# H3 convolution layer with a squared-ReLU MLP on one core: a normalisation moved one step, side jobs of the convolution placed anew, SyncE's transfers held back to three in flight

## The chip, the core and the metric

The kernel runs on one core of a Trainium2 chip. The core has TensorE (PE in the profile; PEld is its weight load), VectorE (DVE), ScalarE (ACT), GpSimd (POOL) and SyncE (SP, which here only issues transfers). The engines run side by side, each through its own list of instructions in order, and wait for each other by semaphores. The metric is the device time of one execution in microseconds, as the median of several runs.

## The reference, cut to what matters

S = 2048 positions, D = 640 channels, F = 1728 hidden units, float32.

```python
mod = (silu(c) @ w_mod)            # six rows of 640: sa, ca, ga, sb, cb, gb
h  = layernorm(x) * (1 + ca) + sa
k_shift = causal_conv(k, shift_k)  # 4 taps per channel
kv = k_shift * v
y  = irfft(rfft(kv, 4096) * rfft(ssm_k, 4096))[:2048] + kv * ssm_D
x  = x + ga * (h * y)              # the long convolution, gated with h
h  = layernorm(x) * (1 + cb) + sb
x  = x + gb * (relu(h @ w1 + b1) ** 2 @ w2 + b2)
```

## The kernel before, in words

**The convolution** takes the channels in five blocks of 128 (b = 0 to 4). The long convolution is a Fourier transform of 4096 points, done as matmuls with constant tables. For each block TensorE runs units of work:

- kv_k, kv_v (L232, L270): transposes of k and v to channels by time, in four pieces of 512. kv_s (L253) applies the taps on VectorE, kv_m (L281) multiplies by v and stores the piece to kv_d in DRAM.
- load_h, load_x (L205, L213): four transfers each bring kv (from kv_d) and ssm_k into the tile p, in another layout.
- unit_a (L374), eight for each block: the first stage of the transform, 64 small matmuls each, "pa" in the profile; four read the ssm_k part of p (i = 1), four the kv part (i = 0). ScalarE copies the result to the tile a.
- front (L421), eight steps j: the second stage for ssm_k (h) and kv (x), the product of the spectra on VectorE (tile wx), sums on GpSimd. back (L449), "qp", turns two steps back.
- unit_t and unit_y (L524, L534), eight each: transposes t and the last inverse stage y, into the tile up.

**Side jobs** are done for the blocks before and after, between these units: the modulation rows (part_load, part_scale, part_add, mod_row, mod_col: load a 128 by 640 piece of w_mod, scale it on ScalarE, add on GpSimd, sum with a matmul by ones), the statistics of the first normalisation (q_big loads q, stats1, stats1_end), the normalised and modulated input (load_xp, prep_a on ScalarE, prep_m on VectorE, prep_p on GpSimd), the gate, the residual (finish_near, finish_add, which stores to x1_d), and the first MLP weights (load_item, w_high on ScalarE, w_low: a weight is split into a high and a low part).

**The order is written out by hand.** A block has ten steps FS(b, 0) to FS(b, 9), with the fronts and backs, and 18 slots GS(b, 0) to GS(b, 17) (11 in the last block). The table filled by at (L890) says which side jobs are called in which step or slot. UNITS (L1069) gives for each block the slots of unit_a for the next block (one more stands in step 9), of unit_t and of unit_y. AFTER (L1067) lists the steps and slots in which the side jobs and the next unit_a change places: normally a slot calls its unit_a first and its side jobs then, in AFTER the other way round. keep_order (L118) ties each engine's instructions to the order in which the program made them.

**Transfers** nearly all go through sp_dma (L137): SyncE issues them in program order, and each waits until the one OUT = 4 places ahead has landed. The pieces of w_mod and the MLP weights share four buffers (tag STG).

**The MLP** goes through 8 chunks n of 256 positions and 14 steps f each (128 hidden units a step). A pass of the main loop at (n, f) calls, in this order: mlp_back of the step three passes ago (MLAG = 3; second matmul, "acc"), mlp_split of the last step (high part on ScalarE, L146, low part on VectorE, L157), mlp_front (first matmul, "h", L720), mlp_front_end (ReLU on ScalarE, L752, the square on GpSimd), and then the work for chunk n + 1: load_x1 at f = 3, stats2 at 5, stats2_root and stats2_end at 6, prep_hat (L670, its ScalarE instruction at L672) and, from f = 8 on, prep_xt, which transposes one block of channels a step (L685, two transposes, one for each half of the chunk, "xtp") and makes its high and low parts. prep_hat(n + 1, i) normalises half i of the next chunk into the tile xh[i] ("mtmp" in the profile); it is called for i = 0 at f = 7 and i = 1 at f = 8, for n = 0 at 5 and 6. xh is also the buffer in which mlp_end and mlp_out scale and add a chunk's result, at f = 2.

Of the kernel before, what the change touches and what calls it, by code (L numbers as in the profile page):

```python
# [28 lines left out]
OUT = 4  # L29
# [63 lines left out]
def ssm_mlp_kernel(  # L93
# [796 lines left out]
    def at(i, *calls):  # L890
        tab[i] += calls
# [45 lines left out]
    def b2_load():  # L937
# [3 lines left out]
    at(FS(0, 1), (kv_k, 1, 0, "T"), (kv_v, 1, 0), (p_tile, 2))  # L941
    at(FS(0, 2), (early_h, 0, 6))
    at(FS(0, 3), (kv_s, 1, 0))
    at(FS(0, 4), (early_h, 0, 7))
    at(FS(0, 5), (kv_m, 1, 0), (kv_k, 1, 1, "T"))
    at(FS(0, 6), (skip, 1))
    at(FS(0, 7), (kv_s, 1, 1))
# [3 lines left out]
    at(GS(0, 1), (kv_s, 1, 2))  # L951
    at(GS(0, 2), (stats1, 0))
    at(GS(0, 3), (kv_m, 1, 2), (kv_k, 1, 3, "X"), (kv_s, 1, 3))
    at(GS(0, 5), (kv_v, 1, 3), (kv_m, 1, 3), (kv_k, 2, 0, "X"), (stats1, 4))
    at(GS(0, 6), (stats1, 1), (mod_start,))
    at(GS(0, 7), (stats1, 2), (part_load, 2, 0), (part_load, 2, 1), (part_load, 2, 2))
    at(GS(0, 8), (load_x, 1), (kv_s, 2, 0), (q_big, "X1", 8))
    at(GS(0, 9), (kv_v, 2, 0), (kv_k, 2, 1, "Y"), (stats1, 3))
    at(GS(0, 11), (kv_m, 2, 0), (stats1, 5))
    at(GS(0, 12), (q_big, "X1", 10))  # L960
    at(GS(0, 13), (kv_s, 2, 1), (kv_v, 2, 1), (kv_m, 2, 1))
    at(GS(0, 14), (load_h, 2), (stats1, 6))
    at(GS(0, 15), (part_load, 2, 3))
    at(FS(1, 0), (part_scale, 2, 1))
    at(FS(1, 1), (kv_k, 2, 2, "T"), (q_big, "UP1", 12), (stats1, 7))
    at(FS(1, 2), (part_scale, 2, 0))
    at(FS(1, 3), (skip, 2), (kv_s, 2, 2), (kv_v, 2, 2), (kv_m, 2, 2), (kv_k, 2, 3, "T"), (part_add, 2, 1, pool))
    at(FS(1, 4), (kv_s, 2, 3), (kv_v, 2, 3), (part_scale, 2, 2), (part_load, 2, 4))
    at(FS(1, 5), (kv_m, 2, 3), (part_add, 2, 2, pool), (part_scale, 2, 3), (part_load, 1, 0))
    at(FS(1, 6), (q_ut,))  # L970
    at(FS(1, 7), (part_add, 2, 3, pool))
    at(FS(1, 8), (load_xp, 0))
    at(FS(1, 9), (load_x, 2), (stats1, 13), (part_scale, 2, 4))
    at(GS(1, 0), (p_tile, 3), (kv_k, 3, 0, "Y"))
    at(GS(1, 1), (kv_s, 3, 0), (part_load, 1, 1))
    at(GS(1, 2), (kv_v, 3, 0), (part_scale, 1, 0))
    at(GS(1, 3), (kv_m, 3, 0), (part_add, 2, 4, pool), (part_load, 1, 2))
    at(GS(1, 4), (kv_k, 3, 1, "Y"), (stats1, 12), (part_load, 1, 4))
    at(GS(1, 5), (kv_v, 3, 1), (stats1, 14), (mod_row, 2), (part_scale, 1, 1), (part_load, 1, 3))
    at(GS(1, 7), (kv_s, 3, 1), (stats1, 15), (part_add, 1, 1, pool))  # L980
    at(GS(1, 8), (kv_k, 3, 2, "Y"))
    at(GS(1, 9), (kv_m, 3, 1), (kv_s, 3, 2), (part_scale, 1, 2), (part_scale, 1, 4), (part_load, 0, 2))
    at(GS(1, 10), (kv_v, 3, 2))
    at(GS(1, 11), (kv_k, 3, 3, "Y"), (stats1, 9), (part_scale, 1, 3), (part_load, 0, 0))
    at(GS(1, 12), (stats1, 11), (part_add, 1, 4, pool), (part_load, 0, 1))
    at(GS(1, 13), (kv_m, 3, 2), (kv_s, 3, 3), (part_add, 1, 2, pool))
    at(GS(1, 14), (kv_v, 3, 3), (part_add, 1, 3, pool))
# [8 lines left out]
    at(FS(2, 4), (part_add, 0, 4, pool), (prep_a, 0, 0), (prep_a, 0, 3), (prep_m, 0, 1))  # L996
    at(FS(2, 5), (prep_m, 0, 0))
    at(FS(2, 6), (skip, 3), (part_load, 3, 0), (part_load, 3, 2), (prep_a, 0, 2), (prep_m, 0, 3))
    at(FS(2, 7), (mod_row, 0), (prep_p, 0, 0), (prep_p, 0, 1))
    at(FS(2, 8), (prep_m, 0, 2))  # L1000
    at(FS(2, 9), (part_load, 3, 1), (prep_p, 0, 2), (prep_p, 0, 3), (gate, 0, 0))
    at(GS(2, 0), (kv_k, 4, 0, "Y"), (part_scale, 3, 0))
    at(GS(2, 1), (kv_s, 4, 0), (part_scale, 3, 1), (gate, 0, 1))
    at(GS(2, 2), (p_tile, 4), (load_h, 4), (part_load, 3, 3), (gate, 0, 3), (finish_add, 0, 1))
    at(GS(2, 3), (kv_v, 4, 0), (kv_m, 4, 0), (kv_k, 4, 1, "Y"), (kv_v, 4, 1))
    at(GS(2, 4),
        (part_scale, 3, 2), (part_load, 3, 4), (gate, 0, 2), (finish_near, 0, 0), (finish_near, 0, 1),
        (finish_add, 0, 2), (finish_add, 0, 3), (prep_a, 1, 0),
    )
# [36 lines left out]
    at(GS(3, 13), (mod_col, 4, cbs[:, 1], 1.0), (prep_m, 3, 2), (prep_p, 3, 2))
    at(GS(3, 15), (prep_m, 3, 1), (prep_p, 3, 1), (w_tile, "S0", 3), (w_low, dve))
    at(GS(3, 16), (w_high,))
    at(GS(3, 17), (prep_a, 3, 3), (w_low, dve))
    at(FS(4, 0), (prep_m, 3, 3), (load_item,), (load_item,))  # L1050
    at(FS(4, 1), (prep_p, 3, 3), (gate, 3, 1), (gate, 3, 2))
    at(FS(4, 2), (gate, 3, 0), (u_tile, 4), (prep_a, 4, 0), (prep_m, 4, 0), (w_high,))
    at(FS(4, 3), (gate, 3, 3), (prep_a, 4, 1))
    at(FS(4, 4), (prep_m, 4, 1), (prep_p, 4, 0), (w_high,))
    at(FS(4, 5), (gate_load,), (load_item,))
    at(FS(4, 6), (prep_a, 4, 2), (w_low, dve))
    at(FS(4, 7), (prep_m, 4, 2), (prep_p, 4, 1))
    at(FS(4, 8), (w_tile, "S2", 3), (w_high,), (w_high,))
    at(FS(4, 9), (finish_add, 3, 1), (w_tile, "S3", 3), (load_item,), (load_item,), (w_low, dve))
    at(GS(4, 0), (prep_a, 4, 3), (prep_m, 4, 3), (prep_p, 4, 2), (prep_p, 4, 3))  # L1060
    at(GS(4, 2), (finish_near, 3, 0), (finish_near, 3, 1), (finish_add, 3, 2))
    at(GS(4, 3), (b2_load,), (w_low, pool), (w_low, pool))
    at(GS(4, 4), (load_item,))
# [203 lines left out]
```

## Time and profile before

| | us |
|---|---|
| median of 3 runs | 703.28 |
| lowest, highest | 702.06, 704.84 |
| profiled execution | 705.5 |
| its span, first to last instruction | 703.7 |

The profile describes one execution. The convolution takes some 285 us of the span and the MLP the rest. A row of the timeline gives start, duration, engine, source line, operation, tiles written and read, shapes, how many alike, and in brackets how long the engine stood idle before it and what ended that. A row of waits gives who waited for whom, the total, how often and the longest. "issue" names idle time that nothing in the profile ended. q1 is the queue of SyncE's transfers, q8 carries instructions (packets, MB, share of the DMA engines' time). Ends of matmuls are modelled, so idle times of TensorE are good to some tenths of a microsecond.

### The profile page before, as it was taken

What the parts mean: (1) busy time and instruction counts of PE and PEld (TensorE: products, weight loads), DVE (VectorE), ACT (ScalarE), POOL (GpSimd) and SP (SyncE); (2) the same over time, 40 slices, a digit from 0 to 9 for tenths busy, and PEclk for the clock granted to TensorE, in tenths of its full rate; (3) what the DMA queues carried; (4) which work ended last, traced back from release to release, by engine and by line L of the source; (5) the groups of instructions that cost most, each with busy time, mean ns of one, the idle gap of its engine ahead of it and who ended that gap; (6) DMA issues with size and microseconds to landing.
All of it is one profiled execution on the core that took longest, in us unless ns stands there. A gap on an engine that the chain in (4) does not pass through costs nothing.

```text
span 703.7 us, 21084 instructions
## 1 busy us (share of the span) xinstructions
PE 662.0 (94%) x9164; PEld 634.2 (90%) x9164; DVE 334.6 (48%) x601; ACT 329.6 (47%) x688; POOL 311.2 (44%) x390
## 2 busy tenths in 40 slices
PE   6699799999999989999999999999999999999997
PEld 5688788888898888899999999999999999999996
DVE  5257666657684886587522323323332322422313
ACT  4436556877967966566233333233233233233221
POOL 1053155459869859433514414315215215224213
PEclk9999999999999999999999999999999999999999
DMA  9887889798672645274010100200200200200001
GB/s 232 248 240 235 238 238 250 232 231 219 181 186 82 158 126 172 69 227 142 39 38 1 42 35 1 74 3 1 75 1 1 76 1 1 76 1 1 38 1 38
DMA packets 110960, 74.76 MB, mean 106 GB/s; under 512 B 48658, under 2 KB 96146, under 8 KB 110868
## 3 DMA queue, kind: packets, MB, share of 16 engines
q1 hardware_dynamic: 108912, 72.87, 36.5%
q8 instruction: 72, 1.18, 0.7%
q10 hardware_dynamic: 1892, 0.54, 0.3%
q14 instruction: 20, 0.16, 0.1%
q0 software_dynamic: 64, 0.01, 0.0%
HBM read 58.98 MB, written 14.42 MB: 104 GB/s over the span
## 4 chain that ended last, share of the span: by engine, by line
PE 83%; ACT 6%; DVE 5%; issue 3%; DMA 2%; POOL 1%; SPq 0%; DVEq 0%; ACTq 0%; POOLq 0%
PE acc L790 27%; PE h L720 25%; PE pa L383 5%; PE x L398 5%; PE qp L464 5%; PE y L541 5%; PE h L398 3%; PE t L530 2%; PE h L711 1%; PE xtp L685 1%; PE kt L239 1%; DVE wx L151 1%; ACT a L146 1%; PE vt L276 1%; PE gr L928 1%
## 5 line engine op out<-in xcount | busy, mean ns | idle before, releaser
L151 POOL TENSOR_TENSOR mtmp<-mtmp 128x256 f32<-128x256 f32 x112 | 71.4, 638 | 244.4 <-ACT mtmp L752 236.5
L720 PE MATMUL h<-xt,w_S 128*128 128x256 f32 x1290 | 167.5, 281 | 1.1 <-DVE w_S L157 1.1
L720 PEld LDWEIGHTS h<-xt,w_S 128*128 128x128 f32 x1290 | 161.7, 190 | 1.3 <-DVE w_S L157 1.3
L790 PE MATMUL acc<-w_S,hring 128*128 128x320 f32 x960 | 156.6, 311 | 0.2 <-DVE hring L157 0.2
L157 DVE TENSOR_TENSOR hring<-mtmp,hring 128x256 fp32r<-128x256 f32 x112 | 66.4, 593 | 162.6 <-ACT hring L146 162.6
L790 PEld LDWEIGHTS acc<-w_S,hring 128*128 128x128 f32 x960 | 142.0, 188 | 0.7 <-DVE hring L157 0.7
L752 ACT ACTIVATE mtmp<-h,b1t 128x256 f32<-128x256 f32 x104 | 49.4, 475 | 180.1 <-PE h L720 177.0
L146 ACT ACTIVATE hring<-mtmp 128x256 fp32r<-128x256 f32 x112 | 46.6, 416 | 48.5 <-POOL mtmp L151 47.5
L383 PE MATMUL pa<-wx,p 64*64 64x64 f32 x2560 | 49.7, 228 | 10.9 <-issue 5.3
L383 PEld LDWEIGHTS pa<-wx,p 64*64 64x64 f32 x2560 | 44.1, 141 | 17.2 <-issue 11.3
L146 ACT ACTIVATE a<-pa 128x512 f32<-128x512 f32 x80 | 43.6, 611 | 22.9 <-PE pa L383 22.8
L151 DVE TENSOR_TENSOR wx<-x,wx 128x512 f32<-128x512 f32 x64 | 41.0, 684 | 19.4 <-PE x L398 8.9
L541 PE MATMUL y<-wx,wx 128*64 128x64 f32 x1280 | 45.4, 226 | 4.5 <-ACT wx L146 2.7
L541 PEld LDWEIGHTS y<-wx,wx 128*64 128x64 f32 x1280 | 40.7, 139 | 9.5 <-issue 4.2
L687 DVE TENSOR_SCALAR we<-xtp,cbs 128x256 f32<-128x256 f32 x35 | 19.0, 544 | 61.1 <-PE xtp L685 61.1
L398 PE MATMUL x<-a,gb 128*64 128x128 f32 x640 | 43.8, 281 | 3.0 <-DVE wx L151 1.8
L398 PEld LDWEIGHTS x<-a,gb 128*64 128x64 f32 x640 | 37.7, 141 | 4.4 <-PE h L398 2.4
L261 DVE SCALAR_TENSOR_TENSOR KV<-kt,tap,KV 128x511 f32<-128x511 f32 (+2 forms) x48 | 35.9, 747 | 8.1 <-ACT ktail L146 6.3
L154 POOL TENSOR_TENSOR wm<-wm,wm 128x640 f32<-128x640 f32 x20 | 32.9, 1647 | 10.3 <-ACT wm L341 10.0
L146 ACT ACTIVATE q<-qp 128x512 f32<-128x512 f32 (+1 forms) x40 | 21.3, 585 | 33.1 <-PE qp L464 33.1
L157 POOL TENSOR_TENSOR we<-wx 128x256 f32<-128x256 f32 x20 | 15.8, 789 | 47.0 <-DVE wx L151 46.1
L398 PE MATMUL h<-a,gb 128*64 128x128 f32 x512 | 34.4, 275 | 0.6 <-ACT wx L146 0.6
(142 smaller groups left out, 1032.7 us busy)
## 6 DMA issues: line engine op xcount, KB each, us to landing
wm<-in_w_mod_dram SPq DMA_DIRECT2D x25, 320.0 KB, 4.2
KV<-in_A_k_dram SPq DMA_DIRECT2D x20, 256.0 KB, 4.6
KV<-in_A_v_dram SPq DMA_DIRECT2D x20, 256.0 KB, 4.5
p<-in_A_ssm_k_dram SPq DMA_DIRECT2D x20, 256.0 KB, 4.9
p<-kv_d SPq DMA_DIRECT2D x20, 256.0 KB, 4.8
xp<-in_A_q_dram SPq DMA_DIRECT2D x20, 256.0 KB, 4.5
q<-in_A_q_dram SPq DMA_DIRECT2D x15, 320.0 KB, 5.0
out_dram<-x SPq DMA_DIRECT2D x14, 320.0 KB, 2.2
```

What stands on the lines that cost most here:

```text
L146: act.activation(o, i, AF.Copy)
L151: eng.tensor_mul(o, a, b)
L154: eng.tensor_add(o, a, b)
L157: eng.tensor_sub(o, a, b)
L261: dve.scalar_tensor_tensor(o, tk[:, : 512 - t], tap[:, b, t : t + 1], o, op0=ALU.mult, op1=ALU.add)
L383: pe.matmul(t[e][64 * r : 64 * r + 64, g].rearrange("p m d -> p (m d)"), pt[b][l, i, 8 * q + g, :], cw[l, r], start=True, stop=True,)
L398: pe.matmul(t[64 * a : 64 * a + 64, s + r], gb[:, g, r, a], AX[b][i][:, 2 * g + a], start=True, stop=True,)
L464: pe.matmul(t[a][:, u], gi[l, 4 * j + u, r], w[r][l, u % 2], start=(r == 0), stop=(r == 1),)
L541: pe.matmul(y[64 * h : 64 * h + 64, 4 * (g % 2) + i].rearrange("p c l d -> p (c l d)"), tss[g][:, i, 64 * r : 64 * r + 64], ca[:, r, h], s ...
L720: pe.matmul(hps[n, f][:m], WI[1, f][:, a, b], XT[n][:, x, b], start=(b == 0 and i == 0), stop=(b == NB - 1 and i == 2),)
L752: act.activation(r[:m], h[:m], AF.Relu, bias=b1t[:m, f : f + 1])
L790: pe.matmul(acc[2 * s + i], h[:, a, s * P : (s + 1) * P], w[:, y, i * 320 : (i + 1) * 320], start=(f == 0 and ti == 0), stop=(f == NF - 1 ...
```

## The change

Three things. (1) OUT is 3: each of SyncE's transfers waits for the third one ahead. (2) In the MLP, for n of 1 and more, both calls of prep_hat stand at f = 7; for n = 0 they stay at 5 and 6. (3) The table of side jobs, UNITS and AFTER are new. All side jobs are still called once each; with them their transfers move in SyncE's order. The diff, cut to its core (of the table those lines that are spoken of below, lines with other jobs of the same step included):

```diff
-OUT = 4
+OUT = 3
...
-    at(FS(0, 8), (kv_v, 1, 1))
-    at(FS(0, 9), (q_big, "XP0", 0))
-    at(GS(0, 0), (kv_m, 1, 1), (kv_k, 1, 2, "Y"), (kv_v, 1, 2), (q_big, "XP1", 4))
+    at(FS(0, 5), (skip, 1), (kv_k, 1, 1, "T"), (q_big, "XP0", 0))
+    at(GS(0, 0), (kv_v, 1, 1), (kv_m, 1, 1), (kv_k, 1, 2, "Y"), (kv_v, 1, 2))
+    at(GS(0, 2), (q_big, "XP1", 4))
...
-    at(FS(1, 8), (load_xp, 0))
-    at(FS(1, 9), (load_x, 2), (stats1, 13), (part_scale, 2, 4))
+    at(GS(1, 1), (load_x, 2), (kv_s, 3, 0), (part_load, 1, 1))
...
-        (kv_m, 3, 3), (stats1, 8), (stats1, 10), (mod_row, 1), (part_scale, 0, 0), (part_scale, 0, 1),
-        (part_scale, 0, 2), (part_load, 0, 3), (part_load, 0, 4),
+        (kv_v, 3, 3), (kv_m, 3, 3), (mod_row, 1), (part_scale, 0, 0), (part_scale, 0, 1), (part_scale, 0, 2),
     )
-    at(GS(1, 16), (load_x, 3), (stats1_end,), (part_add, 0, 1, pool), (part_add, 0, 2, pool))
-    at(FS(2, 0), (load_h, 3), (load_xp, 1))
-    at(FS(2, 2), (part_scale, 0, 3), (prep_a, 0, 1))
-    at(FS(2, 3), (part_add, 0, 3, pool), (part_scale, 0, 4))
+    at(GS(1, 16), (stats1, 8), (part_add, 0, 2, pool), (part_load, 0, 4))
+    at(GS(1, 17), (load_h, 3), (stats1, 10), (load_xp, 1))
+    at(FS(2, 0), (load_x, 3), (part_scale, 0, 3))
+    at(FS(2, 1), (stats1_end,), (part_add, 0, 1, pool), (part_add, 0, 3, pool), (prep_a, 0, 1))
+    at(FS(2, 2), (part_scale, 0, 4))
...
-    at(FS(4, 0), (prep_m, 3, 3), (load_item,), (load_item,))
-    at(FS(4, 2), (gate, 3, 0), (u_tile, 4), (prep_a, 4, 0), (prep_m, 4, 0), (w_high,))
-    at(FS(4, 4), (prep_m, 4, 1), (prep_p, 4, 0), (w_high,))
+    at(GS(3, 17), (prep_p, 3, 1), (u_tile, 4), (w_low, dve), (load_item,))
+    at(FS(4, 2), (gate, 3, 0), (prep_a, 4, 1), (prep_m, 4, 0), (w_high,), (w_high,))
...
     UNITS = [
-        ([0, 2, 4, 11, 11, 16, 16], [1, 3, 3, 5, 5, 6, 7, 9], [3, 4, 4, 6, 6, 8, 9, 10]),
-        ([1, 1, 5, 7, 9, 10, 12], [1, 3, 4, 6, 8, 11, 14, 14], [4, 6, 7, 10, 13, 14, 16, 17]),
+        ([0, 1, 4, 11, 13, 16, 16], [1, 3, 3, 5, 5, 6, 7, 9], [3, 4, 4, 6, 7, 8, 8, 11]),
+        ([2, 2, 5, 5, 10, 10, 12], [1, 4, 4, 7, 8, 11, 13, 14], [4, 7, 7, 11, 13, 13, 16, 17]),
...
-                if f - (5 if n == 0 else 7) in (0, 1):
-                    prep_hat(n + 1, f - (5 if n == 0 else 7))
+                if n == 0 and f in (5, 6):
+                    prep_hat(1, f - 5)
+                if n and f == 7:
+                    prep_hat(n + 1, 0)
+                    prep_hat(n + 1, 1)
```

AFTER goes from 20 places to 27. In the built program the new order gives TensorE of block 1 three pairs of unit_a with nothing between them (slots 2, 5 and 10), where there was one (slot 1).

More of the change, by code (lines that the diff above doesn't have):

```diff
@@ new lines, in ssm_mlp_kernel @@
+    at(GS(0, 2), (q_big, "XP1", 4))
+    at(GS(0, 3), (kv_m, 1, 2), (kv_k, 1, 3, "X"), (kv_s, 1, 3), (stats1, 4))
+    at(GS(0, 5), (kv_v, 1, 3), (kv_m, 1, 3), (kv_k, 2, 0, "X"), (stats1, 1))
+    at(GS(0, 6), (stats1, 3), (mod_start,), (part_load, 2, 0))
+    at(GS(0, 7), (kv_s, 2, 0), (stats1, 2), (part_load, 2, 2))
+    at(GS(0, 8), (load_x, 1))
+    at(GS(0, 9), (kv_v, 2, 0), (stats1, 5), (part_load, 2, 1))
+    at(GS(0, 10), (kv_k, 2, 1, "Y"))
+    at(GS(0, 11), (kv_m, 2, 0), (kv_s, 2, 1), (q_big, "X1", 8))
@@ L1059, in ssm_mlp_kernel @@
[L1059 to L1063, printed above, removed]
-    at(GS(4, 5), (finish_add, 3, 3), (gate_vector,), (load_item,))
-    AFTER = {GS(0, 9), GS(0, 11), GS(0, 14), GS(1, 1), GS(1, 4), GS(1, 12), GS(1, 13), GS(1, 14), FS(2, 9), GS(2, 1), GS(2, 2), GS(2, 9), GS(2, 10), GS(2, 15), GS(2, 17), GS(3, 2), GS(3, 5), GS(3, 10), GS(3, 12), GS(3, 16)}
@@ L1069, in ssm_mlp_kernel @@
-    UNITS = [
[5 rows of a table removed]
+    at(GS(2, 9), (kv_s, 4, 2), (kv_v, 4, 2), (part_add, 3, 2, pool), (part_add, 3, 3, pool))
+    at(GS(2, 10), (load_xp, 2), (prep_m, 1, 1))
+    at(GS(2, 11), (kv_k, 4, 3, "Y"), (part_scale, 3, 4))
+    at(GS(2, 12), (part_add, 3, 4, pool), (prep_p, 1, 1), (prep_a, 1, 2))
+    at(GS(2, 13), (kv_m, 4, 2), (kv_s, 4, 3), (kv_v, 4, 3))
+    at(GS(2, 14), (kv_m, 4, 3))
+    at(GS(2, 15),
+        (mod_col, 3, cbs[:, 0], 0.0), (prep_m, 1, 2), (prep_a, 1, 3), (prep_m, 1, 3), (prep_p, 1, 3),
+        (gate, 1, 0),
+    )
@@ new lines, in ssm_mlp_kernel @@
+    at(GS(2, 16), (part_load, 4, 3), (prep_p, 1, 2), (gate, 1, 1))
+    at(GS(2, 17), (part_load, 4, 1))
+    at(FS(3, 0), (part_load, 4, 2), (finish_near, 1, 1), (prep_a, 2, 0))
+    at(FS(3, 1), (part_load, 4, 0), (gate, 1, 2), (finish_near, 1, 0))
+    at(FS(3, 2), (load_x, 4), (finish_add, 1, 2))
+    at(FS(3, 3), (skip, 4))
+    at(FS(3, 4), (part_scale, 4, 0), (gate, 1, 3), (prep_m, 2, 0), (prep_p, 2, 0))
+    at(FS(3, 5), (finish_add, 1, 1))
+    at(FS(3, 6), (part_scale, 4, 1), (part_scale, 4, 2))
@@ new lines, in ssm_mlp_kernel @@
+    at(FS(3, 7), (prep_a, 2, 1))
+    at(FS(3, 8), (part_add, 4, 2, pool), (gate, 2, 0))
+    at(FS(3, 9), (part_scale, 4, 3), (prep_m, 2, 1))
+    at(GS(3, 1), (part_add, 4, 1, pool), (finish_add, 1, 3), (prep_p, 2, 1))
+    at(GS(3, 2), (part_load, 4, 4), (prep_a, 2, 2))
+    at(GS(3, 3), (prep_m, 2, 2), (prep_a, 2, 3), (finish_near, 2, 0), (w_tile, "S1", 3))
+    at(GS(3, 4), (part_add, 4, 3, pool), (load_xp, 3), (prep_p, 2, 2))
+    at(GS(3, 5), (prep_m, 2, 3), (prep_p, 2, 3), (gate, 2, 1), (finish_near, 2, 1))
@@ new lines, in ssm_mlp_kernel @@
+    at(GS(3, 6), (load_item,))
+    at(GS(3, 7), (load_item,))
+    at(GS(3, 8), (part_scale, 4, 4))
+    at(GS(3, 9), (part_add, 4, 4, pool), (gate, 2, 2), (finish_add, 2, 2), (prep_a, 3, 0), (b1_load,))
+    at(GS(3, 10), (finish_add, 2, 1), (prep_a, 3, 2), (load_item,))
+    at(GS(3, 11), (prep_m, 3, 0), (w_high,))
+    at(GS(3, 12),
+        (mod_col, 4, cbs[:, 1], 1.0), (gate, 2, 3), (finish_add, 2, 3), (load_xp, 4), (prep_p, 3, 0),
+        (prep_a, 3, 1),
+    )
+    at(GS(3, 13), (prep_m, 3, 2))
@@ new lines, in ssm_mlp_kernel @@
+    at(FS(4, 5), (prep_m, 4, 1))
+    at(FS(4, 6), (prep_a, 4, 2), (gate_load,))
+    at(FS(4, 7), (prep_m, 4, 2), (prep_p, 4, 1))
+    at(FS(4, 8), (finish_add, 3, 1), (w_tile, "S3", 3), (w_high,))
+    at(FS(4, 9), (prep_a, 4, 3), (prep_p, 4, 2), (w_tile, "S2", 3), (w_low, dve))
+    at(GS(4, 0), (prep_m, 4, 3), (prep_p, 4, 3))
+    at(GS(4, 1), (finish_add, 3, 2), (load_item,), (load_item,), (w_high,))
+    at(GS(4, 2), (finish_near, 3, 0), (finish_near, 3, 1))
+    at(GS(4, 3), (b2_load,))
```

156 lines of the change are left out of this document (61 added, 95 removed), and 6 rows, old and new, of the table UNITS.

## The prediction, as put on record before the run

> **What bounds the kernel now.** I read the page first: its busy shares, the slices, the chain that ended last.
>
> ```profile
> span 703.7 us, 21084 instructions
> PE 662.0 (94%) x9164; PEld 634.2 (90%) x9164; DVE 334.6 (48%) x601; ACT 329.6 (47%) x688; POOL 311.2 (44%) x390
> ...
> DMA  9887889798672645274010100200200200200001
> ...
> q8 instruction: 72, 1.18, 0.7%
> ...
> PE 83%; ACT 6%; DVE 5%; issue 3%; DMA 2%; POOL 1%; SPq 0%; DVEq 0%; ACTq 0%; POOLq 0%
> ```
>
> TensorE carries the chain almost alone, so a change is worth what it does to TensorE's waits. Transfers fill the first third of the span and nearly vanish later. The profiled execution took 705.5 us, 1.8 more than its span; the median of the runs shown is 703.28 (702.06 to 704.84). I make the sum on the 705.5 and subtract it from the median as well.
>
> Second view: who waited for whom on TensorE, in two stretches. First 300 to 703 us (the MLP; matmul row, then weight load row), then 36 to 300 us (convolution). Columns: total us, times, longest.
>
> ```profile
> PE xtp L685 <- ACT mtmp L672: 7.9, 6, 1.3
> PEld xtp L685 <- ACT mtmp L672: 9.3, 6, 1.6
> ```
> ```profile
> PE pa L383 <- issue: 4.7, 4, 2.3
> PE y L541 <- ACT wx L146: 2.7, 4, 1.3
> PE y L541 <- issue: 1.8, 3, 1.0
> PE x L398 <- DVE wx L151: 1.8, 3, 1.0
> PE x L398 <- ACT a L146: 1.1, 1, 1.1
> PE t L530 <- DVE q L148: 0.6, 1, 0.6
> PE h L398 <- ACT wx L146: 0.6, 1, 0.6
> PE kt L239 <- ACT q L146: 0.5, 1, 0.5
> ```
>
> The MLP has one wait that comes back: six times TensorE's transposes (L685) wait for ScalarE's normalisation (L672). The convolution has 6.5 us of waits named issue (nothing shown ends them) and about 8 us of short waits for ScalarE, VectorE and others, each once to four times. The three parts of the change aim at these three lists.
>
> **Part 1, the second normalisation a step sooner.** TensorE around the first of the six, at step f = 8 of chunk 1, then ScalarE:
>
> ```profile
> 369.92 0.27 PE L685 MATMUL xtp<-ident,mtmp 128*128 128x128 f32 x1
> 371.51 0.33 PE L685 MATMUL xtp<-ident,mtmp 128*128 128x128 f32 x1 [1.32 <-ACT mtmp L672]
> ...
> 375.24 0.38 PE L685 MATMUL xtp<-ident,mtmp 128*128 128x128 f32 x2
> ...
> 379.02 0.38 PE L685 MATMUL xtp<-ident,mtmp 128*128 128x128 f32 x2
> ```
> ```profile
> 367.02 0.91 ACT L672 ACTIVATE mtmp<-x,nm,rs 128x640 f32<-128x640 f32 x1
> 367.85 0.42 ACT L146 ACTIVATE hring<-mtmp 128x256 fp32r<-128x256 f32 x1
> 370.18 0.47 ACT L752 ACTIVATE mtmp<-h,b1t 128x256 f32<-128x256 f32 x1 [1.91 <-PE h L720]
> 370.55 0.91 ACT L672 ACTIVATE mtmp<-x,nm,rs 128x640 f32<-128x640 f32 x1
> ```
>
> The first transpose (tile xh[0]) runs at 369.92; the second (xh[1]) needs the second normalisation, which stands behind the ReLU of step 8, and that ReLU waits for step 8's own matmuls. So it starts at 370.55 and TensorE stands still. How long: the step with the wait lasts 375.24 - 369.92 = 5.32 us, the next, equal but for the wait, 379.02 - 375.24 = 3.78. The difference is 1.54, six times 9.2 us (the weight load row says 9.3, the matmul row 7.9, which are my two bounds).
>
> After the change both normalisations stand at step 7: 367.02 + 2 x 0.91 = 368.84, 1.1 us before the transpose at 369.92. The same instructions run; nothing is added. What is pushed: the high-half copy of step 7 goes from 367.85 to about 368.8, and VectorE's low half behind it. Its reader is the second matmul of step 7, three steps on (MLAG = 3), some 10 us. ScalarE is free again before the ReLU at 370.18. The second normalisation needs no input later than the first, which starts at 367.02 with no wait, and its buffer was last read in mlp_out at step 2. What is late next: step 9's transposes, which already run without a wait at 375.24. I take **-9.2** (bounds -9.3 and -7.9). For chunk 1 the code is the same as before, so six, not seven.
>
> **Part 2, three transfers ahead instead of four.** The wait sits on SyncE; behind it stand all loads and stores, in program order. Two effects.
>
> Instruction loads. The pa rows stop in mid-unit. Here two such rows of TensorE, the DMA row of 86.5 to 88.0 us, and the one of 380 to 400 us.
>
> ```profile
> 88.85 0.80 PE L383 MATMUL pa<-wx,p 64*64 64x64 f32 x38 [2.31 <-issue]
> ```
> ```profile
> 134.51 0.91 PE L383 MATMUL pa<-wx,p 64*64 64x64 f32 x43 [1.33 <-issue]
> ```
> ```profile
> q8 instruction: 1, 0.02, 3.9%
> ```
> ```profile
> q8 instruction: 2, 0.03, 0.7%
> ```
>
> The stall ends at 88.85, and one instruction load (0.02 MB) moves between 86.5 and 88.0, inside it. In the MLP, where almost nothing else moves, the same loads come and the list of 300 to 703 us has no issue wait. So I read issue here as TensorE out of instructions because their load stands behind data. The queue is one transfer shorter now. One transfer is worth 1.1 us (below), so the 2.31 falls to 1.2, the 1.33 to 0.2, and the five others (2.9 us in all, 1.0 the longest) go: at most -5.0. Against it: TensorE's new order sets three pairs of pa units back to back in block 1 (slots 2, 5, 10) where one stood (slot 1), and such runs are where TensorE starves; two more stalls of 1.33 are +2.7. Between -5.0 and +2.7 I take **-2.0**: nearer the gain, as the rows show the stall with the load in it, but not half of the most.
>
> The Trainium skill, DMA: Bandwidth & Descriptors, section Queues, rings and completion order, speaks against this term: each DMA engine takes turns between queue rows at packet granularity, so an instruction load would not wait for the data row's depth. By it the term is 0 or, with the pairs, positive; it is rival B. The trace leans against it, with the load arriving only inside a 2.31 us stall, but no row here shows the load's own waiting time.
>
> Throughput. The rows: a transfer with three others ahead (page, median of 20), one issued at 24.7 us with nothing in flight, and the three windows from 36 to 160 us (the last columns are DMA share and GB/s).
>
> ```profile
> KV<-in_A_k_dram SPq DMA_DIRECT2D x20, 256.0 KB, 4.6
> ```
> ```profile
> p<-kv_d SPq DMA_DIRECT2D x1, 256.0 KB, 2.9
> ```
> ```profile
> 36.00:80.00 44.00, 41.11 (x839) 37.60 (x840) 28.42 (x52) 20.43 (x41) 16.97 (x35) 0.93 0.81 236
> 80.00:120.00 40.00, 37.06 (x902) 33.83 (x901) 26.34 (x50) 23.32 (x44) 20.34 (x35) 0.99 0.88 246
> 120.00:160.00 40.00, 37.49 (x878) 33.41 (x877) 26.10 (x53) 31.17 (x59) 21.47 (x27) 1.00 0.88 231
> ```
>
> 236 x 44 + 246 x 40 + 231 x 40 is 29.5 MB in 124 us, 112 pieces of 256 KB, 1.1 us each. Three in flight keep that pace as long as one lands within 3.3 us of its issue; alone it takes 2.9. So the margin is thin but there, and most of the 4.6 is queueing that goes with the fourth. The first chain of loads (0 to 36 us) has no other work beside it; I charge it **+0.3**, between 0 and 1 (one 1.1 us transfer late once).
>
> **Part 3, the side jobs.** All of them remain, with the same instructions: counts by engine do not change, only places. Hidden work that stays hidden costs nothing; so I look at the waits it makes or takes away. One clear case, ScalarE at the start of block 2 (two rows), then TensorE:
>
> ```profile
> 145.14 1.56 ACT L341 ACTIVATE wm<-wm,sg 128x640 f32<-128x640 f32 x2 [1.36 <-DMA wm<-in_w_mod_dram]
> 146.72 1.28 ACT L303 ACT_TABLE_LOAD   x1
> ```
> ```profile
> 149.36 1.09 PE L398 MATMUL h<-a,gb 128*64 128x128 f32 x16 [0.55 <-ACT wx L146]
> 150.78 1.09 PE L398 MATMUL x<-a,gb 128*64 128x128 f32 x16 [0.32 <-DVE wx L151]
> ```
>
> stats1_end (table load and root) sits between late weight scalings and the copies of h: TensorE loses 0.87. It moves from slot 16 of block 1 to step 1 of block 2, after two copies. -0.87 if the copies then keep ahead; but prep_a(0, 1) now follows in the same step and waits on ScalarE for VectorE's reciprocal, so the wait may return. Second case, a wait that may be new: load_x(2) goes two slots later (FS(1, 9) to GS(1, 1)), and the unit that reads it, pa of block 1, two slots sooner (7 to 5).
>
> ```profile
> 117.08 4.88 SPq L138 DMA_DIRECT2D p<-kv_d  x4
> ```
> ```profile
> 128.33 1.16 PE L383 MATMUL pa<-wx,p 64*64 64x64 f32 x64
> ```
>
> Now the last of the four is issued by 121.96 and, with 2.9 to 4.6 us to land, is there by 124.9 to 126.6, before 128.33. Moved 2 slots of some 2 us each, with the unit as much sooner, the first quarter comes about when it is needed: 0 to +2.3 (two units of 1.16). Third, ScalarE's scaling of wm_0_4 (FS(2, 2) instead of FS(2, 3), its load one slot later) and the copy of w2s_1 (FS(4, 2) instead of FS(4, 4)) come nearer to their loads. ScalarE's waits for transfers from 36 to 300 us are now:
>
> ```profile
> ACT wm L341 <- DMA wm<-in_w_mod_dram: 2.9, 3, 1.4
> ACT KV L241 <- DMA kv_d<-KV: 2.7, 1, 2.7
> ```
>
> Each of the two may wait like the 1.4, ahead of h copies. So the whole part lies between -5 (most of the 8 us) and +5 (2.3 and two of 1.4); I take **-0.5**, near nothing, since for most of the short waits the order of ScalarE and TensorE around them stays as it was.
>
> **Sum.** -9.2 - 2.0 + 0.3 - 0.5 = -11.4: 705.5 becomes 694.1, the median 703.3 becomes **691.9 us**.
>
> **The rivals.**
>
> B. Instruction loads do not come sooner, or the new pairs eat the gain. For it: the pairs, and the DMA share of 0.81 to 0.88, which leaves gaps in which a load could move whatever stands in line: then it is late by its own landing time, not by the queue. Against: the load inside the stall. (The section cited points to B.) Term 0 to +2.7 instead of -2.0: 693.9 to 696.6, say 695.3. Chance 0.20.
>
> C. The moved side jobs cost what the loads save: the late p quarter, ScalarE held by wm_0_4 and w2s_1, in all +8 against forecast, 699.9. For it: waits of ScalarE for transfers of 1.4 and 2.7 us happen now. Against: the 8 us of present waits are many small ones, and no engine but TensorE is busy above half. Chance 0.08.
>
> D. Slower: SyncE's stream becomes bound by the landing time. If a transfer takes T with three in flight, the pace is T/3, and 112 pieces pay. Up to 3.3 us nothing is lost; at 3.64 the pace is 1.21 and 11.4 us are gone if all of it reaches TensorE, at 3.73 the kernel is slower by 0.5%. At T = 4.2 the pace is 1.4, the stretch 33 us longer; with half of it exposed the kernel takes 708.4. For it: 4.6 now, share 0.81 to 0.88. Against: a lone transfer takes 2.9. Chance 0.05.
>
> E. Part 1 does not do what it says: the transposes wait for something else at once (a store of xh, the low half), and only 2 us in all are won: 701.3. Against: 1.1 us of slack and no other reader. Chance 0.05.
>
> **How the numbers follow.** A has 0.62 and goes from 687 (9.2 with -5.0 and -2) to 694.5. To leave out no more than 0.2 the range takes in B whole and C's lower part: 686.5 to 699.0. Two measurements of this kernel can be told apart from about 0.5% on (3.5 us): faster means under 699.8. A, B and a quarter of C's and E's chance are faster: 0.85. Same: 0.10. Slower, D: 0.05.
>
> **What would show it.** Step 1: no wait of xtp for L672 in the MLP, and a step 8 of 3.8 us; a wait that stays refutes it. Step 2: issue waits of pa and y under 4.5 us in all, landings of KV loads about 3.3 to 3.6 us; over 6.5 speaks for B, landings over 3.7 for D. Step 3: the pair 149/151 gone, no wait of pa for p<-kv_d in block 1. I would be wrong above all if ScalarE's waits for transfers grew over the 2.9 and 2.7 us above and showed as h and y waits on TensorE.

## The result and the profile after

The changed kernel takes 706.9 us (median of 20 runs, 703.7 to 713.2), the kernel before 703.3 (20 runs, 700.9 to 707.7). The ratio is 1.0056, with a 95% interval of 1.0032 to 1.0079: some 4 us slower, where 11.4 us faster was predicted. The profiled execution took 708.63 us, its span is 706.9.

First the MLP, where part 1 works: all rows that the list of TensorE's waits has from 300 us on, then the transposes of chunk 1's steps 8 and 9 (start, duration, ..., idle time before).

```profile
PE h L720 <- DVE w_S L157: 1.1, 1, 1.1
PE acc L790 <- DVE hring L157: 0.2, 1, 0.2
```
```profile
382.32 0.38 PE L685 MATMUL xtp<-ident,mtmp 128*128 128x128 f32 x2
386.10 0.38 PE L685 MATMUL xtp<-ident,mtmp 128*128 128x128 f32 x2
```

The wait of xtp for L672 is gone, and step 8 takes 386.10 - 382.32 = 3.78 us, as a step without the wait did before. From this transpose to the end of the span it was 703.7 - 369.92 = 333.8 us and is 706.9 - 382.32 = 324.6: 9.2 us less. But the transpose itself comes 382.32 - 369.92 = 12.4 us later. So the MLP won just what was forecast, and the convolution lost 12.4 us. Its page: DMA share in tenths, GB/s, and the chain of waits; then two landings (median from issue to landing).

```profile
DMA  8887887878875374427220020020010100200001
GB/s 202 231 230 235 222 222 212 213 223 208 206 202 143 90 186 150 137 70 239 66 76 1 1 75 2 1 75 1 35 41 1 58 19 1 76 1 1 38 1 38
...
PE 68%; DMA 22%; ACT 3%; DVE 3%; POOL 2%; issue 1%; SPq 0%; POOLq 0%; ACTq 0%; DVEq 0%
```
```profile
KV<-in_A_k_dram SPq DMA_DIRECT2D x20, 256.0 KB, 4.2
p<-kv_d SPq DMA_DIRECT2D x20, 256.0 KB, 3.9
```

The share of transfers on the chain went from 2% to 22%. Each transfer lands sooner (4.2 us for the KV loads, 4.6 before), and yet less moves: of the first ten slices (to 177 us) nine stand 8 to 38 GB/s lower than before, and only about a quarter of what was not moved there follows in the next two (206 and 202 against 181 and 186); the rest comes later still. The prediction had named landings of 3.3 to 3.6 us for itself and over 3.7 for rival D. Now who waits, from 36 to 300 us: TensorE, then ScalarE for transfers.

```profile
PE pa L383 <- DMA p<-kv_d: 5.8, 1, 5.8
PE y L541 <- ACT wx L146: 3.6, 2, 3.4
PE x L398 <- DVE wx L151: 2.9, 5, 1.1
PE pa L383 <- issue: 2.6, 3, 1.2
PE mc L350 <- ACT wx L146: 2.1, 1, 2.1
PE kt L239 <- DMA KV<-in_A_k_dram: 1.2, 1, 1.2
```
```profile
ACT KV L241 <- DMA kv_d<-KV: 13.4, 6, 4.8
ACT wm L341 <- DMA wm<-in_w_mod_dram: 5.7, 5, 2.8
```

TensorE has three new long waits (5.8, 3.4, 2.1). They cost more than their length. Here is TensorE's unit behind the longest one, then the stretch of 120 to 160 us (the third number from the end is TensorE's granted clock):

```profile
131.93 1.99 PE L383 MATMUL pa<-wx,p 64*64 64x64 f32 x64 [5.77 <-DMA p<-kv_d]
```
```profile
120.00:160.00 40.00, 33.03 (x855) 29.08 (x853) 21.57 (x44) 24.37 (x45) 15.06 (x20) 0.91 0.77 218
```

The unit takes 1.99 us where the same 64 matmuls took 1.16 before, and the clock of this stretch is 0.91 where it was 1.00. Read in windows of 2 us, it falls to 0.5 at about the end of each of the three waits and stays there for 3 to 7 us: some 17 us in all between 36 and 300 us, where it was some 7 before.

ScalarE stands 13.4 us before the taps of a k piece (L241), whose buffer an earlier piece's store has not yet left; before, these waits were 2.7 us. Two theories follow. **T**: three in flight are too few, SyncE's stream of transfers goes slower, falls behind, and whatever needs it next waits (rival D of the prediction). **J**: the new places of the side jobs make the waits, load_x(2) and its reader above all (rival C, the "second case").

### The profile page after: what moved, and what is told of

It reads as the page before. It is cut to its first block, busy times and chain, and to the rows that moved or that the text cites. A ratio compares the mean times of both kernels' runs of the same rounds, so it can differ in the third digit from the quotient of the medians.

```text
span 706.9 us, 21091 instructions
## 1 busy us (share of the span) xinstructions
PE 662.5 (94%) x9164; PEld 635.4 (90%) x9164; DVE 334.5 (47%) x601; ACT 330.1 (47%) x688; POOL 311.7 (44%) x390
## 3 DMA queue, kind: packets, MB, share of 16 engines
q8 instruction: 72, 1.18, 0.7%
## 4 chain that ended last, share of the span: by engine, by line
PE 68%; DMA 22%; ACT 3%; DVE 3%; POOL 2%; issue 1%; SPq 0%; POOLq 0%; ACTq 0%; DVEq 0%
PE acc L790 27%; PE h L720 25%; DMA KV<-in_A_k_dram 5%; DMA wm<-in_w_mod_dram 3%; DMA kv_d<-KV 3%; PE y L541 3%; PE qp L464 2%; DMA q<-in_A_q_dram 2%; DMA p<-kv_d 2%; DMA p<-in_A_ssm_k_dram 2%; PE x L398 2%; PE h L398 2%; PE pa L383 2%; PE h L711 1%; PE xtp L685 1%
## 5 line engine op out<-in xcount | busy, mean ns | idle before, releaser
L541 PEld LDWEIGHTS y<-wx,wx 128*64 128x64 f32 x1280 | 43.6, 148 | 9.4 <-ACT wx L146 4.5
L541 PE MATMUL y<-wx,wx 128*64 128x64 f32 x1280 | 47.8, 235 | 4.4 <-ACT wx L146 3.6
L398 PE MATMUL x<-a,gb 128*64 128x128 f32 x640 | 41.6, 274 | 5.2 <-DVE wx L151 2.9
L398 PEld LDWEIGHTS x<-a,gb 128*64 128x64 f32 x640 | 35.7, 137 | 7.3 <-PE h L398 2.7
L790 PE MATMUL acc<-w_WX,hring 128*128 128x320 f32 x192 | 31.4, 312 | 0.0
```

What stands on the lines that cost most here:

```text
L398: pe.matmul(t[64 * a : 64 * a + 64, s + r], gb[:, g, r, a], AX[b][i][:, 2 * g + a], start=True, stop=True,)
L541: pe.matmul(y[64 * h : 64 * h + 64, 4 * (g % 2) + i].rearrange("p c l d -> p (c l d)"), tss[g][:, i, 64 * r : 64 * r + 64], ca[:, r, h], s ...
L790: pe.matmul(acc[2 * s + i], h[:, a, s * P : (s + 1) * P], w[:, y, i * 320 : (i + 1) * 320], start=(f == 0 and ti == 0), stop=(f == NF - 1 ...
```

## The experiments

Each run was timed beside the kernel before on the same chip. The last column is (ratio - 1) times 703.3. The ratio is not the quotient of the medians; by these the column would differ by up to 1.9 us (e9 would be +2.7, e13 +3.1, e14 +2.2), which is within the intervals.

| kernel | median us | ratio, 95% interval | us against before |
|---|---|---|---|
| changed kernel | 706.9 | 1.0056, 1.0032 to 1.0079 | +3.9 |
| e1: part 1 alone, four ahead | 694.1 | 0.9871, 0.9833 to 0.9909 | -9.1 |
| e2: part 1, three ahead | 703.3 | 1.0004, 0.9976 to 1.0032 | +0.3 |
| e3: changed, four ahead | 693.6 | 0.9861, 0.9824 to 0.9899 | -9.8 |
| e4: part 1, five ahead | 698.9 | 0.9929, 0.9894 to 0.9963 | -5.0 |
| e5: part 1, 3 / 4 / 4 ahead | 697.6 | 0.9915, 0.9885 to 0.9945 | -6.0 |
| e6: part 1, 4 / 3 / 4 ahead | 702.2 | 0.9983, 0.9962 to 1.0005 | -1.2 |
| e7: part 1, 4 / 4 / 3 ahead | 693.5 | 0.9851, 0.9821 to 0.9880 | -10.5 |
| e8: changed, load_x(2) back | 707.9 | 1.0066, 1.0039 to 1.0094 | +4.6 |
| e9: e8 and its reader back | 706.6 | 1.0065, 1.0036 to 1.0094 | +4.6 |
| e10: e2 with halves of 512 KB | 699.8 | 0.9960, 0.9934 to 0.9986 | -2.8 |
| e11: part 1, six ahead | 698.1 | 0.9916, 0.9889 to 0.9943 | -5.9 |
| e12: changed, 4 / 4 / 3 ahead | 695.6 | 0.9900, 0.9859 to 0.9941 | -7.0 |
| e13: changed, block 2's slots old | 705.6 | 1.0026, 0.9993 to 1.0058 | +1.8 |
| e14: e2, block 2's slots new | 704.6 | 1.0013, 0.9977 to 1.0049 | +0.9 |

### The parts one by one: e1 to e4

e1 is the kernel before with this alone; e2 and e4 are e1 with OUT = 3 and 5; e3 is the changed kernel with OUT = 4.

```diff
-                if f - (5 if n == 0 else 7) in (0, 1):
-                    prep_hat(n + 1, f - (5 if n == 0 else 7))
+                if n == 0 and f in (5, 6):
+                    prep_hat(1, f - 5)
+                if n and f == 7:
+                    prep_hat(n + 1, 0)
+                    prep_hat(n + 1, 1)
```

> Part 1 alone, the rest as before: the second normalisation joins the first at step 7. Both theories expect the same: the six waits of xtp for L672 go and nothing else moves, -9.2 us, 694 us against 703.3 before. Over 698 would say that the MLP's gain is paid for in the convolution by part 1 itself, which the code gives no reason for.

> Parts 1 and 2, side jobs of before. Theory T (three in flight starve SyncE's stream: a landing of about 4.0 us divided by 3 is a pace of 1.33 us for 256 KB instead of 1.1): most of the 12.4 us that the convolution lost comes from here, so 703 to 706 us and convolution landings of 3.9 to 4.2 us. Theory J (the new places cost it, load_x(2) above all): 693 to 695 us, the convolution as long as before or 2 us shorter.

> Parts 1 and 3: the changed kernel with four transfers ahead again. Theory T: 692 to 697 us, the wait of pa for p<-kv_d is gone or under 2 us. Theory J: 703 to 707 us, and the wait of pa for p<-kv_d stays about 6 us, since load_x(2) is still issued two slots later and read two slots sooner.

> Part 1, side jobs of before, five transfers ahead. Theory T: the stream at four in flight moves about 240 GB/s at best in its busy slices; if that is still bound by the landing time, five are a gain of 1 to 5 us over part 1 alone (689 to 693 us); if four already fill the DMA engines, no change (within 1.5 us of part 1 alone) with landings some 1.1 us longer. The prediction's view of instruction loads (they wait behind data) expects longer issue waits than with four, +1 to +3 us. Theory J says nothing about it.

Measured: part 1 alone gives 9.1 us. With it, the new places at four ahead give 0.7 us more (-9.8 against -9.1, not told apart from nothing by the intervals). Three ahead cost 9.4 us with the old places and 13.7 with the new ones. J falls as the main cause, T holds. How T works is seen by putting e1 beside e2, which differ in nothing but OUT. For each first the stretch of 36 to 160 us (busy time and instructions of TensorE, its weight loads, VectorE, ScalarE, GpSimd; last TensorE's clock, DMA share and GB/s) and the landing of a KV load, then two of SyncE's rows: in both kernels the first row begins with transfer 48, counted from 0, and the second with transfer 102.

e1, four ahead:

```profile
36.00:160.00 124.00, 116.49 (x2662) 105.87 (x2664) 82.05 (x156) 77.84 (x149) 61.41 (x98) 0.99 0.87 243
```
```profile
KV<-in_A_k_dram SPq DMA_DIRECT2D x20, 256.0 KB, 4.3
```
```profile
63.41 3.70 SPq L138 DMA_DIRECT2D q<-in_A_q_dram  x4
```
```profile
124.10 1.69 SPq L138 DMA_DIRECT2D wm<-in_w_mod_dram  x2
```

e2, three ahead:

```profile
36.00:160.00 124.00, 110.90 (x2523) 99.98 (x2517) 77.67 (x148) 70.28 (x132) 53.77 (x90) 0.96 0.80 228
```
```profile
KV<-in_A_k_dram SPq DMA_DIRECT2D x20, 256.0 KB, 3.7
```
```profile
66.33 1.77 SPq L138 DMA_DIRECT2D q<-in_A_q_dram  x3
```
```profile
135.63 1.08 SPq L138 DMA_DIRECT2D wm<-in_w_mod_dram  x2
```

With four ahead 54 transfers take 124.10 - 63.41 = 60.7 us, 1.12 each; with three 135.63 - 66.33 = 69.3 us, 1.28 each. The lag grows from 2.9 to 11.5 us. The fourth transfer took only 0.6 us of landing with it when it went (4.3 to 3.7), and 3.7 / 3 is 1.23 where 4.3 / 4 is 1.08: each landed sooner, but three such slots carry less than four. Where the lag reaches TensorE is seen in two rows of e2, ScalarE's and TensorE's:

```profile
134.89 0.83 ACT L341 ACTIVATE wm<-wm,sg 128x640 f32<-128x640 f32 x1 [7.90 <-DMA wm<-in_w_mod_dram]
```
```profile
136.27 0.78 PE L239 MATMUL kt<-ident,KV 128*128 128x128 f32 x4 [4.76 <-ACT up L146]
```

A piece of w_mod is late; ScalarE stands 7.9 us before it, in order, and cannot copy y out; TensorE stands 4.76 us before its next transpose, which needs the buffer. Its next unit then takes 1.99 us instead of 1.16:

```profile
136.97 1.99 PE L383 MATMUL pa<-wx,p 64*64 64x64 f32 x64
```

So a part of the price is not waiting but a slower TensorE. Over all runs the median granted clock is 0.993 in e1 and 0.9875 in e2; it is 0.993 in e3 and 0.985 in the changed kernel. (The kernel before has 0.9945 beside e1, e2 and e3.) Times 700 us, the difference is 3.9 us of the 9.4 and 5.6 of the 13.7: an estimate, as if TensorE were busy throughout. The rows show the slow stretches behind the long waits; no run holds the clock and changes the waits alone.

Five ahead (e4) are no gain but by the ratios a loss of 4.1 us against e1, though the two intervals overlap a little. Its stretch and landing, and its issue waits from 36 to 160 us; then those of e1.

```profile
36.00:160.00 124.00, 115.36 (x2600) 104.28 (x2600) 79.94 (x152) 74.25 (x141) 58.12 (x95) 0.97 0.84 232
```
```profile
KV<-in_A_k_dram SPq DMA_DIRECT2D x20, 256.0 KB, 4.9
```
```profile
PE pa L383 <- issue: 3.6, 2, 2.1
PE y L541 <- issue: 0.3, 1, 0.3
```
```profile
PE pa L383 <- issue: 1.0, 1, 1.0
PE y L541 <- issue: 0.7, 1, 0.7
```

The fifth adds 0.6 us of landing and no throughput: here four are enough to fill the stream. The issue waits are 3.9 instead of 1.7 us, but with four ahead the kernel before has 3.9 in this stretch too, and e3 has 5.5: these single profiles do not show that a deeper queue makes them longer. The median granted clock is 0.989 against 0.993 in e1, by the same estimate 2.8 us; why it is lower stays open.

### Where three ahead cost: e5, e6, e7

e1 with the depth by the number n of the transfer. With 3, 4, 4 it is e5, with 4, 3, 4 e6, with 4, 4, 3 e7.

```diff
-        if len(queued) > OUT:
+        n = len(queued) - 1
+        ahead = 3 if n < 48 else 4 if n < 110 else 4
+        if n >= ahead:
...
-            tc.add_manual_dep(nc.cur_bb.bb.instructions[-1], queued[-1 - OUT], info, reason="place in time")
+            tc.add_manual_dep(nc.cur_bb.bb.instructions[-1], queued[-1 - ahead], info, reason="place in time")
```

> Part 1, side jobs of before; three transfers ahead for the first 48 transfers alone (issued up to 63 us), four after. Theory T (a pace of the stream: in the run with three throughout, transfer 48 was issued 2.9 us late and transfer 102 11.5 us late, so the lag grows by 0.17 us with every transfer while the stream is full): the lag stays at 2 to 3 us, TensorE loses 1 to 3, so 695 to 697 us. Rival P (each wait costs a fixed price, 9.2 us over 243 transfers): 48 of them are 1.8 us, 696 us. This one alone does not tell them apart; the next two do.

> The same with three ahead for transfers 48 to 109 alone (63 to about 140 us). Theory T: the lag grows by 9 us here, TensorE loses 5 to 8 of it: 699 to 702 us. Rival P: 62 transfers of 243, 2.3 us: 696.4 us.

> The same with three ahead for transfers 110 to 242 alone (from about 140 us on). Theory T: the stream is no longer full from 160 us on (179 of some 250 GB/s), so little is lost, and instruction loads come sooner: TensorE won back 2 us after 140 us in the run with three throughout: 691.5 to 694.5 us. Rival P: 133 of 243 transfers, 5 us: 699 us.

Against e1 the three stretches cost +3.1, +7.9 and -1.4 us; their sum, 9.6, is the 9.4 of three throughout. A fixed price for each wait (P) would have put the most into the third stretch, with 133 of 243 transfers, and there nothing is lost. By the intervals only e6 is clear of e1; e5 and e7 are not. But e7 is also clear of P's 699 us. The price is paid where the stream is full. The stretch from 160 to 300 us in e1, for comparison:

```profile
160.00:300.00 140.00, 133.91 (x2932) 121.86 (x2926) 101.59 (x153) 98.55 (x210) 109.98 (x110) 1.00 0.54 148
```

A DMA share of 0.54 and 148 GB/s, against 0.87 and 243 from 36 to 160 us: here three slots are enough.

### Whether the places matter: e8, e9

e8 moves the four loads of kv back, e9 their first reader as well.

```diff
-    at(FS(1, 9), (part_scale, 2, 4))
+    at(FS(1, 9), (load_x, 2), (part_scale, 2, 4))
-    at(GS(1, 1), (load_x, 2), (kv_s, 3, 0), (part_load, 1, 1))
+    at(GS(1, 1), (kv_s, 3, 0), (part_load, 1, 1))
```
```diff
-        ([2, 2, 5, 5, 10, 10, 12], [1, 4, 4, 7, 8, 11, 13, 14], [4, 7, 7, 11, 13, 13, 16, 17]),
+        ([2, 2, 5, 7, 10, 10, 12], [1, 4, 4, 7, 8, 11, 13, 14], [4, 7, 7, 11, 13, 13, 16, 17]),
```

> The changed kernel with load_x(2) back at FS(1, 9), where before had it; three ahead. The places and the depth together cost 4.1 us more than each alone (706.9 - 703.3 and 693.6 - 694.1). If the late load_x(2) is that interaction: the wait of pa for p<-kv_d of 5.8 us shrinks to under 2 and the time is 702 to 704 us. If the stream's lag decides whatever the order (pure T): the four loads take the place of four others, which are late instead, and the time stays at 706 to 708 us.

> The changed kernel, three ahead, with both sides of the meeting as before: load_x(2) at FS(1, 9) and its first reader, the unit pa of block 2, at slot 7 of block 1 instead of 5 (two slots, some 4 to 5 us later). If the 4.1 us that places and depth cost together are this meeting: 702 to 704 us, the wait of pa for p<-kv_d under 2 us. If the late stream takes the time somewhere else anyway: 706 to 708 us, with the wait gone and another in its place.

Both stay at the changed kernel's time. In e8 the wait of pa is still there; in e9, with both sides back, 0.36 us of it are left, and just after that unit ScalarE stands before a late piece of w_mod and TensorE behind it. TensorE's row of e8, then ScalarE's and TensorE's of e9:

```profile
130.67 1.98 PE L383 MATMUL pa<-wx,p 64*64 64x64 f32 x64 [5.37 <-DMA p<-kv_d]
```
```profile
137.77 1.55 ACT L341 ACTIVATE wm<-wm,sg 128x640 f32<-128x640 f32 x2 [8.65 <-DMA wm<-in_w_mod_dram]
```
```profile
139.86 1.11 PE L239 MATMUL kt<-ident,KV 128*128 128x128 f32 x4 [5.57 <-ACT up L146]
```

5.8, 5.4, 5.6 us: in these three profiles the order of the jobs decides who waits for the late stream, not how long.

### Data or places in the queue: e10; more depth: e11; a split for the changed kernel: e12

```diff
-    def load_h(b, n=4):
+    def load_h(b, n=2):
...
-    def load_x(b, n=4):
+    def load_x(b, n=2):
...
-        for l in range(0, NL, 4):
-            sp_dma(t[:, l : l + 4], src[:, l : l + 4])
+        for l in range(0, NL, 8):
+            sp_dma(t[:, l : l + 8], src[:, l : l + 8])
```

That is e10, on e2. e11 is e1 with OUT = 6. e12 is the changed kernel with four ahead up to transfer 109 and three from 110 on, written as in e7.

> Part 1, side jobs of before, three ahead, but the loads of p and xp in halves of 512 KB instead of quarters of 256 KB (60 transfers become 30). If what counts is the data in flight (theory T by bytes): the pace comes back toward that of four, 695 to 700 us. If what counts is the number of transfers ahead whatever their size (each slot blocks SyncE in program order): 703 us, or slower, since the first reader of each p tile now waits for the larger half.

> Part 1, side jobs of before, six ahead. Four gave 694.1, five 698.9. Theory I (the stream is full with four, and every further transfer in flight delays the instruction loads of TensorE; with five the issue waits at two pa units grew by 1.1 and 1.5 us): another 2 to 5 us, 701 to 704 us, issue waits over 8 us. If five cost something else that happens once (one changed place in the order of two waits): as with five, 697 to 700 us.

> Parts 1 and 3, four ahead for the first 110 transfers and three after. Theory T: the stream is not full from about 150 us on, so this keeps the 693.6 of four throughout and may win the 0.6 that the same split won with the side jobs of before: 692 to 694 us. If the new places need the fourth transfer later as well (the lag of the changed kernel grew from 11 us at 138 to 16 us at 187): 695 to 699 us.

e10: with the same three slots but larger pieces the kernel is 3.1 us faster than e2 (the intervals, 0.9934 to 0.9986 and 0.9976 to 1.0032, overlap at their ends). A landing and the stretch of 36 to 160 us:

```profile
p<-kv_d SPq DMA_DIRECT2D x10, 512.0 KB, 6.0
```
```profile
36.00:160.00 124.00, 111.74 (x2645) 100.99 (x2637) 77.52 (x148) 72.65 (x136) 53.43 (x90) 0.96 0.82 232
```

Twice the data lands in 6.0 us where 256 KB took 3.9 in e2, as in the changed kernel: less than twice the time, so a part of the landing does not grow with the size. It fits that the data in flight counts, and a third of the loss came back this way. e11: six cost as much as five, not more; the expectation that each further slot costs 2 to 5 us failed, and the issue waits from 36 to 300 us were 6.6, not over 8. e12's median lies where its text puts new places that need the fourth transfer later as well, but its interval overlaps that of e3 (0.9859 to 0.9941 against 0.9824 to 0.9899): neither case is shown, and what e7 hinted at is no gain here.

### The rest of the places: e13, e14

The new places cost nothing at four ahead, but 3.6 us at three (+3.9 against +0.3; by the two intervals 3.6 could be 1 to 6). The 4.1 of the expectations is these 3.6 plus the 0.5 by which the medians put the new places ahead at four. The 2.1 us wait of mc above stands in block 2's slots. e13 puts there the old jobs and units into the changed kernel, e14 the new ones into e2; of the 18 slots, those around the wait:

```diff
-    at(GS(2, 13), (kv_m, 4, 2), (kv_s, 4, 3), (kv_v, 4, 3))
-    at(GS(2, 14), (kv_m, 4, 3))
-    at(GS(2, 15),
-        (mod_col, 3, cbs[:, 0], 0.0), (prep_m, 1, 2), (prep_a, 1, 3), (prep_m, 1, 3), (prep_p, 1, 3),
-        (gate, 1, 0),
-    )
-    at(GS(2, 16), (part_load, 4, 3), (prep_p, 1, 2), (gate, 1, 1))
+    at(GS(2, 13), (kv_m, 4, 2), (kv_s, 4, 3), (prep_p, 1, 2))
+    at(GS(2, 14), (kv_v, 4, 3), (prep_a, 1, 3))
+    at(GS(2, 15), (prep_m, 1, 3), (gate, 1, 0))
+    at(GS(2, 16), (mod_col, 3, cbs[:, 0], 0.0), (part_load, 4, 1), (prep_p, 1, 3), (gate, 1, 1))
```

> The changed kernel, three ahead, with the side jobs and t and y units of block 2's slots (GS(2, 0) to GS(2, 17)) as before had them. If the 4.1 us sit there: the wait of mc for L146 goes and the time is 702.5 to 704.5 us. If they come from the late stream as a whole, or from block 0 and 1: 705.5 to 708 us.

> The other way round: part 1, three ahead, side jobs of before except block 2's slots, which are those of the changed kernel. If the 4.1 us sit there: 706 to 708 us against 703.3 with all old places. If not: 702 to 704.5 us.

The wait goes with the slots: e13 has none of mc, e14 has it:

```profile
PE mc L350 <- ACT wx L146: 2.6, 1, 2.6
```

But in e13 a wait of h for ScalarE of 2.2 us, which the changed kernel has not, stands in its list instead. The times moved by -2.1 (e13) and +0.6 us (e14), by the medians -0.6 and +1.7, all within an uncertainty of some 3 us. So these runs do not show how much of the 3.6 us sits in block 2's slots. By the estimate above the clock, 0.9875 in e2 and 0.985 in the changed kernel, is 1.8 of them; where the rest sits stays open.

## Why the prediction was wrong, point by point

**Part 1 (-9.2).** Right, in place and size: 9.2 us in the MLP by the profile, 9.1 in e1.

**Part 2, instruction loads (-2.0).** The direction fits: the issue waits from 36 to 300 us were 6.5 us before and are 2.6 + 0.3 = 2.9 now, under the 4.5 that the prediction named. One profile says little, as e1 and e3, both with four ahead, have 3.9 and 7.4. Over the profiles of one depth throughout, with 256 KB pieces, three ahead have 1.4 to 4.5 us (six of them, mean 2.9; e10 with its larger pieces has 5.2) and four have 3.9 to 7.4 (three, mean 5.9). So the sum fell by some 3 us, near the forecast. That instruction loads wait behind data is not shown by it: with three ahead TensorE also stood longer for other things, and no row has the loads' own waiting time.

**Part 2, throughput (+0.3, between 0 and +1).** This step failed, and it alone turns the sign: the depth costs 9.4 us with the old places and 13.7 with the new, net of what the issue waits gained, where the two terms of part 2 together were forecast at -1.7. The prediction put the price at nothing as long as a landing stays under 3.3 us, took from a lone transfer's 2.9 that it would, and held that "most of the 4.6 is queueing that goes with the fourth". It wasn't: from e1 to e2 only 0.6 us went (4.3 to 3.7), not 1.1. The medians vary with the profile, but with three ahead throughout and 256 KB pieces the KV loads took 3.6 to 4.2 us in all six, with four 4.3 to 4.6 in three; none came under 3.3. Even the +0.3, charged for the first chain of loads, was low: with three ahead for the first 48 transfers alone, e5 costs 3.1 against e1, though by the intervals it could be nothing.

The trace before gave a warning, as the 2.9 was misread. SyncE's row at this transfer:

```profile
24.72 2.88 SPq L138 DMA_DIRECT2D p<-kv_d  x4
```

It had nothing in flight ahead of it, but it is the first of four that were issued within 2.9 us. The other three landed 4.7, 4.9 and 5.0 us after their issue. So the row is not a transfer alone, and beside it three landings stood far above 3.3.

From the KV loads' 3.7, 4.3 and 4.9 us with three (e2), four (e1) and five ahead (e4), a straight line has 0.6 us for each transfer and 1.9 for none. This is an estimate from three medians; e11, with six, has 5.0 and does not lie on the line. It speaks for a fixed part that a shorter queue does not remove and that more data in flight covers. The Trainium skill, DMA: Bandwidth & Descriptors, section Anatomy of one DMA, states a fixed part of about 2.0 us for a DMA issued by GpSimd, most of it the confirmation that the last byte has landed. The estimate of 1.9 us for SyncE's transfers here is close to it, but no run measures that part.

Rival D named the mechanism (pace T/3, 112 pieces, half of it exposed) and nearly the price: 112 times 1.28 - 1.12 is 18 us, half of it 9, and 9.4 were measured. For a T of 4.2, the changed kernel's KV landing, it gave 708.4, and 706.9 came. That this is so close is in part luck: the half was a guess, a part of the loss is the slower clock, which D does not have, and by the changed kernel's 223 GB/s from 36 to 160 us the pace was 1.18 us, not 4.2 / 3 = 1.4. (D's bounds of 3.64 and 3.73 come out some 0.03 lower by its own sum, which changes nothing.) Its chance of 0.05 was too low, for the same reason as the step failed.

**Part 3 (-0.5).** At four ahead the -0.7 between e1 and e3 agrees with it, but the intervals allow some 4 us either way, so it is not confirmed. The first case came out in part: in the changed kernel the 0.55 of h at the start of block 2 is gone, and x waits 0.18 and 0.32 us where it waited 0.32.

```profile
158.41 1.04 PE L398 MATMUL h<-a,gb 128*64 128x128 f32 x16
159.64 1.09 PE L398 MATMUL x<-a,gb 128*64 128x128 f32 x16 [0.18 <-DVE wx L151]
160.71 1.09 PE L398 MATMUL h<-a,gb 128*64 128x128 f32 x16
162.12 1.09 PE L398 MATMUL x<-a,gb 128*64 128x128 f32 x16 [0.32 <-DVE wx L151]
```

The second case, the late quarter of p, was priced 0 to +2.3 and shows 5.8; but e3, with the same places and four ahead, has no such wait at all, and e8 and e9 move it without winning time: this is the stream's lag and not the place alone. The last sentence of the prediction, that it would be wrong above all if ScalarE's waits for transfers grew and showed on TensorE, describes what happened: 5.6 us of them became 19.1 (13.4 and 5.7).

**A version that beats both.** e1, e3 and e7, at 694.1, 693.6 and 693.5 us, are 1.3 to 1.5% faster than before and are not told apart: the normalisation moved, four transfers ahead, side jobs as one likes.

## What to carry to other kernels

A stream of transfers that keeps its engines busy needs its depth: with a landing of a fixed part plus a share for each transfer in flight, taking one away shortens the landing by its share alone, and the pace, landing over depth, gets worse. Read the share from two rows, a lone landing and a landing in the full queue, before calling the last place in the queue mere waiting, and make sure that the lone one has nothing behind it either. When a stream falls behind, don't chase the waits one by one: here moving the job that waits handed the same 5 us to the next one. And look at the granted clock behind a long wait before you price the wait by its length.

## What the runs showed of the hardware that was not expected

Landings of 256 KB KV loads were 3.7, 4.3 and 4.9 us with three, four and five in flight (e2, e1, e4; 5.0 with six, e11), and the full stretch moved 228, 243 and 232 GB/s. 512 KB landed in 6.0 us with three in flight. More than four brought no throughput and cost 3 to 4 us (five -5.0, six -5.9, four -9.1 against before, with intervals that overlap at their ends); what makes them cost is not shown.

From about the end of each of the changed kernel's waits of 5.8, 3.4 and 2.1 us TensorE's granted clock stood at 0.5 for 3 to 7 us, and behind the first a unit of 64 matmuls took 1.99 us instead of 1.16. The median clock of a kernel's runs was 0.993 with four ahead (e1, e3), and 0.9875 (e2) and 0.985 (changed kernel) with three.
